# Where the small products stand in a packed-attention and gated feed-forward kernel, and which PSUM quarter each step writes

## The chip, the cores and the metric

The kernel runs on one core of a Trainium2 chip. The metric is the device time in microseconds of one execution, the median over several runs; lower is better. The core's engines are TensorE (PE; its weight loads are shown apart as PEld), VectorE (DVE), ScalarE (ACT), GpSimd (POOL) and SyncE (SP), which issues the DMAs here. [...]

## The reference

Eight batch entries, eight heads, 576 tokens of head dimension 64, 32 packed tokens; feed-forward width 1024.

```python
def sm_attn(qq, kk, vv):
    s = scale * np.matmul(qq, kk.transpose(0, 1, 3, 2))
    s = s - np.max(s, axis=-1, keepdims=True)
    a = np.exp(s)
    a = a / (np.sum(a, axis=-1, keepdims=True) + 1e-09)
    return np.matmul(a, vv)
p_packed = sm_attn(p, k, v)          # 32 packed tokens attend to 576 tokens
x = sm_attn(q, p_packed, p_packed)   # 576 tokens attend to the 32
...
h = np.maximum(x @ w_in, 0.0)
u, v = (h[..., :d_ff // 2], h[..., d_ff // 2:])
v_n = (v - mu) / np.sqrt(var + 1e-06)
v_s = np.einsum('ts,bsd->btd', w_spatial, v_n) + b_spatial[None, :, None]
return ((u * v_s) @ w_out).astype(np.float32)
```

## The kernel before

The batch is walked entry by entry. While the feed-forward of entry b runs (object `ff`, with the attention results of `att`), the attention of entry b+1 (object `nxt`) is threaded between its steps. Entry 0 and the conversion of the weights form a prologue; `for b in range(1, B)` does the rest. All four compute engines are pinned: each issues its instructions in the order in which the Python code calls them, so the order of the calls is the schedule. The order of the work on one engine is therefore written out by hand, and a waiting instruction holds up everything behind it on its engine.

The steps of one entry, in the order before:

- `pack_scores` (PE): packed-token scores of entry b+1, for r = 0 and r = 1 (heads are numbered 2j + r; r chooses the upper or lower 64 rows of the array). Each r is 2 halves of the columns times 4 heads, 64x32 products of float32, two PE instructions each: 16 instructions per r, 32 in all. `pack_max` (DVE), `pack_exp` (ACT) and `pack_sum` (DVE) follow.
- `value(2)`, `value(0)`, `value(1)` (PE, 512 columns wide): the second half of the feed-forward input. `relu`, `relu_tail`, `stats`, `norm`, `norm_hi`, `norm_lo` (ACT, DVE, POOL) normalise it and split it into high and low parts `v_h`, `v_l`, `v_tail`.
- `pack_turn` (PE transposes), `up(0)`, `pack_values` (PE), `up(1)`, `packed_turn`, `up(2)`, `up(3)`: the first half u of the feed-forward input in four chunks e, between the packed attention's next steps; `up_relu` (ACT) keeps each chunk.
- `query_scores` (PE): scores of the 576 queries against the packed tokens, for r = 0 and r = 1, the same shape as `pack_scores`. `query_max(r)` (DVE) transposes the scores out of PSUM into the tile `sm_t`, takes the maximum and subtracts it; `query_exp` (ACT); `query_norm`, `query_turn` (DVE); `query_hi` (ACT) and `query_lo` (DVE) give `a_h`, `a_l`.
- `gate(e)` for e = 0 to 3 (PE, 28 products of 288 columns each) with `gated(e)` (DVE multiplies by u, ACT makes `g_h`) and `gated_lo(e)` (DVE makes `g_l`).
- `mix(1)`, `mix(0)` (PE): packed tokens times `w_in`, 512 columns, 64x32 products, one call for each half x of `w_in`; `mix_hi` (ACT) and `mix_lo` (DVE) split them into `m_h`, `m_l`. The next entry's `value` needs mix(1), its `up` needs mix(0).
- `down(f)` for f = 0 to 3 (PE, 24 products each, over e = 0 to 3), a copy on ACT into a tile `o`, and a store on SP.

PSUM is divided into two pools of two buffers, each buffer of two banks:

```python
    pa = ctx.enter_context(tc.tile_pool(name="pa", bufs=2, space=bass.MemoryType.PSUM))
    pm = ctx.enter_context(tc.tile_pool(name="pm", bufs=2, space=bass.MemoryType.PSUM))
```

`psum_a` serves the attention steps and `psum_m` the feed-forward; each pool hands its buffers out by turns, and a step that takes a buffer waits until the last reader of its former content is done. In the trace the buffers are named `pa_t` and `pm_t`.

Loads go through SP in the order of the calls: `load_k` (tiles kT and pT), `load_v`, `load_q`; kT, v and qT have one buffer each, so a load waits for the last reader of the former entry's data. All engine calls are recorded under one line of the helper class, L42; so the profile's groups are told apart by tiles.

Of the kernel before, what the change touches and what calls it, by code (L numbers as in the profile page):

```python
# [29 lines left out]
# The high word of float64's 2**-126 (the least normal float32), read as float32.  # L30
# [3 lines left out]
class InOrder:  # L34
    """An engine whose instructions are issued in the order of the trace."""
# [13 lines left out]
def body(ctx: ExitStack, tc, q, k, v, vt, p, w_in, w_sp, b_sp, w_out, out):  # L49
    """Two-stage packed attention followed by the spatially gated feed-forward.  # L50

    Heads are numbered h = 2*j + r. An operand with the head dimension in the
    contraction lies on partition (r, d); one with the packed tokens lies on
    partition (j, n), once per r.

    Every float32 value x that enters a one-pass product is held as two
    float32r values with x == hi + lo exactly; a product is hi*hi + hi*lo +
    lo*hi.
    """
# [14 lines left out]
    def psum_a():  # L74
        return pa.tile([P, 2, 512], F32, tag="pa", name="pa_t")

    def psum_m():
        return pm.tile([P, 2, 512], F32, tag="pm", name="pm_t")
# [94 lines left out]
    # w_spatial: [s, t] in chunks of s; the last chunk holds the remaining rows  # L173
    # twice (for v's hi and lo), and its partner the low parts and the bias.
# [16 lines left out]
    def split_spatial():  # L191
        """Steps, each on the scalar engine and then GpSimd."""
# [29 lines left out]
    def scores(ps, lhs, rhs, rs=(0, 1), by_half=False):  # L222
        for r in rs:
            ps[r] = psum_a()
# [16 lines left out]
    class Attention:  # L241
        """The steps for one batch entry; each is a stage on one engine."""

        def __init__(self, b):
            self.b = b
            self.t, self.at = [None, None], [None, None]

        def pack_scores(self, rs=(0, 1)):
# [6 lines left out]
            scores(self.s1, loaded["p", self.b], loaded["k", self.b], rs, self.b == 0)  # L255
# [27 lines left out]
        def pack_turn(self):  # L283
            p1 = self.p1
            self.p1T = one.tile([P, NC + 1, 2, P], F32, tag="p1T", name="p1T")
            self.t1, self.t2 = psum_a(), psum_a()
# [16 lines left out]
        def pack_values(self):  # L303
            v_sb = loaded.pop(("v", self.b))
            self.pv = psum_a()
# [22 lines left out]
        def packed_turn(self):  # L328
            self.ppt = psum_a()
# [6 lines left out]
        def query_scores(self):  # L336
            self.s2 = {}
            scores(self.s2, self.ppT, loaded.pop(("q", self.b)), by_half=self.b == 0)
# [3 lines left out]
        def query_max(self, r, eng=dve):  # L342
# [3 lines left out]
            )  # L346
            mx = small.tile([P, NM], F32, tag="mx", name="mx")
# [31 lines left out]
        def mix(self, x, rs=(0, 1), psum=psum_a):  # L379
# [3 lines left out]
            self.ms = psum()  # L383
            for r in rs:
                for j in range(NJ):
                    mm(
                        self.ms[32 * j : 32 * j + 32, r, :],
# [6 lines left out]
        def mix_hi(self, x, rs=slice(0, 2)):  # L394
            act.copy(self.m_h[:, x, rs, :], self.ms[:, rs, :])

        def mix_lo(self, x, rs=slice(0, 2)):
            rest(self.m_l[:, x, rs, :], self.ms[:, rs, :], self.m_h[:, x, rs, :])

# [1 line left out]
    class FeedForward:  # L401
        """The steps for one batch entry. g counts pairs of row chunks of v."""

        def __init__(self, b, att):
# [3 lines left out]
            self.gs = {}  # L408
# [94 lines left out]
        def up(self, e, rs=(0, 1)):  # L503
            a_h, a_l, m_h, m_l = self.a_h, self.a_l, self.m_h, self.m_l
            if 0 in rs:
                self.us = psum_m()
            for r in rs:
                for n, (ww, aa) in enumerate(((m_h, a_h), (m_h, a_l), (m_l, a_h))):
                    for x in range(2):
                        mm(  # L510
                            self.us[:, x, :HS],
# [6 lines left out]
        def up_relu(self, e):  # L518
            if e == 0:
                self.u = one.tile([P, NJ, S], F32, tag="u", name="u")  # L520
            act.activation(halves(self.u[:, e, :]), self.us[:, :, :HS], AF.Relu)
# [27 lines left out]
        def gate_keep(self, e):  # L549
            """Where the gate comes before u."""  # L550
# [4 lines left out]
        def gated(self, e, gate_first=False):  # L555
# [5 lines left out]
            if gate_first:  # L561
                dve.scalar_tensor_tensor(
                    halves(g), self.us[:, :, :HS], 0.0, other, op0=ALU.max, op1=ALU.mult
# [8 lines left out]
        def down(self, f, split=False):  # L572
            """The halves of the rows by turns or, if split, one after the other."""
            wout_h, wout_l = wout
            fs = slice(f * P, (f + 1) * P)
            terms = [
                (e, ww, gg)
                for e in range(NJ)
                for ww, gg in ((wout_h, self.g_h), (wout_l, self.g_h), (wout_h, self.g_l))
            ]  # L580
            o = two.tile([P, S], F32, tag="o", name="o")
            for xs in ((0,), (1,)) if split else ((0, 1),):
                ps = psum_a() if 0 not in xs else psum_m()
                for n, (e, ww, gg) in enumerate(terms):
                    for x in xs:
                        mm(
                            ps[:, x, :HS],
                            ww[:, e, fs],
                            gg[:, e, x * HS : (x + 1) * HS],
                            n == 0,  # L590
                            n == len(terms) - 1,
                        )
                ts = slice(xs[0] * HS, (xs[-1] + 1) * HS)
                act.copy(
                    o[:, ts].rearrange("p (x t) -> p x t", t=HS),
                    ps[:, xs[0] : xs[-1] + 1, :HS],
                )
                nc.sync.dma_start(out[f * P : (f + 1) * P, self.b, ts], o[:, ts])

# [1 line left out]
    # Every engine issues in the order of the steps below.  # L601
# [56 lines left out]
    att.query_scores()  # L658
    load_q(1)
    keep_warm(W[5])  # L660
    next(conv_v2)
    att.query_max(0, pool)
    att.query_exp(0)
    att.query_max(1, pool)
# [135 lines left out]
    ff.down(0)  # L800
# [5 lines left out]
    ff.down(1)  # L806
# [9 lines left out]
    ff.down(2)  # L816
    ff.down(3)

# [1 line left out]
    for b in range(1, B):  # L820
        more = b + 2 < B
        att, nxt = nxt, (Attention(b + 1) if b + 1 < B else None)
# [16 lines left out]
        if nxt:  # L839
            nxt.pack_turn()  # L840
# [3 lines left out]
        if more:  # L844
            load_k(b + 2)
        ff.norm(0)
        ff.up(0)
        ff.up_relu(0)
        if nxt:
            ff.norm_hi(0)  # L850
            ff.norm(1)
            nxt.pack_values()
            nxt.packed()
            if more:
                load_v(b + 2)
            ff.norm_lo(0)
            ff.up(1)
            ff.norm_hi(2)
            ff.up_relu(1)
            ff.norm_hi(1)  # L860
            nxt.packed_turn()
            nxt.packed_turned()
        else:
            ff.up(1)
            ff.up_relu(1)
            ff.norm_hi(0)
            ff.norm(1)
            ff.norm_lo(0)
            ff.norm_hi(1)
            ff.norm_hi(2)  # L870
        ff.norm_lo(1)
        ff.up(2)
        ff.up_relu(2)
        ff.norm_lo(2)
        ff.up(3)
        ff.up_relu(3)
        if nxt:
            nxt.query_scores()
            if more:
# [11 lines left out]
        ff.gated_lo(0)  # L891
        ff.gate((1,), psum=psum_m if nxt else psum_a)
        ff.gated(1)
        if nxt:
            nxt.query_lo(0)
# [3 lines left out]
        ff.gated_lo(1)  # L899
        if nxt:  # L900
# [60 lines left out]
```

## Time and profile before

| | |
|---|---|
| median of 3 runs | 439.56 us (438.66 to 440.19) |
| span of the profiled execution, first to last instruction | 438.5 us |
| PE busy | 417.3 us (95%) |
| DVE busy | 290.4 us (66%) |
| ACT busy | 185.1 us (42%) |
| POOL busy | 71.7 us (16%) |
| granted PE clock over the span | 0.983 |
| data read and written | 36.61 MB and 9.44 MB |

Rows of the timeline give start and duration in us, engine, line, operation, output tile<-input tiles, shape, and the number of instructions merged into the row; the bracket tells how long the engine was idle before it and what it waited for. In rows of several matmuls the duration runs to the end of the last one; successive matmuls overlap, so the pace is read from start to start. A row of groups ends in the total busy time and the mean duration in ns. The middle entries repeat every 48.9 us or so; entry 2 starts near 150.4, entry 3 near 199.3, entry 4 near 248.1, and the last, entry 7, near 394.7.

### The profile page before, as it was taken

Reading aid. Unit: us, or ns where it says so; the run is one execution under the profiler, and the core shown is the slowest. Engines: PE = TensorE matmul, PEld = TensorE weight load, DVE = VectorE, ACT = ScalarE, POOL = GpSimd, SP = SyncE. Lnnn points to the kernel's source line nnn. Section 1 sums busy time; section 2 is a strip of 40 time slices with the busy share of each in tenths; the row PEclk is TensorE's granted clock in tenths of the full one; section 3 lists DMA queues with packets and bytes.
Section 4 is the critical chain, followed back from the end, with each engine's and each line's share of the span. In section 5 each row is a group of like instructions: output and inputs, shape, how many; then the busy total and the mean of one; then the engine's idle time right before and its main releaser. Section 6 shows DMA issues by size and latency. Waiting matters only on the chain.

```text
span 438.5 us, 8946 instructions
## 1 busy us (share of the span) xinstructions
PE 417.3 (95%) x3882; PEld 367.6 (84%) x3882; DVE 290.4 (66%) x485; ACT 185.1 (42%) x275; POOL 71.7 (16%) x90
## 2 busy tenths in 40 slices
PE   8968877899999999999999999999999999999997
PEld 6755766787898989897898889897898889898997
DVE  2699988697697177834797187825796278825530
ACT  2364663535634264244634354234534363334411
POOL 1356743400300021001200030001200030002100
PEclk9997996999999999999999999999999999999999
DMA  7997303514330335014330335024320200020002
GB/s 258 359 369 287 104 0 116 210 63 167 111 108 4 121 113 205 1 55 169 110 109 28 120 98 195 1 74 142 127 91 28 82 2 1 0 82 29 0 3 106
DMA packets 14219, 46.61 MB, mean 106 GB/s; under 512 B 1378, under 2 KB 4706, under 8 KB 11364
## 3 DMA queue, kind: packets, MB, share of 16 engines
q1 hardware_dynamic: 14180, 46.05, 29.7%
q8 instruction: 30, 0.49, 0.5%
q14 instruction: 9, 0.07, 0.1%
HBM read 36.61 MB, written 9.44 MB: 105 GB/s over the span
## 4 chain that ended last, share of the span: by engine, by line
PE 73%; DVE 15%; DMA 4%; ACT 3%; issue 2%; POOL 2%; SPq 1%; ACTq 0%; POOLq 0%; DVEq 0%
PE pm_t L42 61%; PE pa_t L42 12%; DMA raw<-in_w_in 4%; DVE bits L42 3%; DVE sm_t L42 2%; DVE sm L42 2%; DVE vr_tail L42 1%; ACT p L42 1%; DVE nmax L42 1%; DVE m_l L42 1%; POOL rstd L42 1%; DVE vn L42 1%; DVE w_in_sb L42 1%; POOL wsp_l L42 1%; DVE g_l L42 1%
## 5 line engine op out<-in xcount | busy, mean ns | idle before, releaser
L42 PE MATMUL pm_t<-g_h,wout_l 128*128 128x288 f32 x252 | 54.4, 296 | 1.1 <-POOL wout_l L42 1.1
L42 PE MATMUL pm_t<-g_h,wout_h 128*128 128x288 f32 x252 | 55.1, 299 | 0.2 <-ACT o L42 0.2
L42 PE MATMUL pm_t<-g_l,wout_h 128*128 128x288 f32 x252 | 54.3, 296 | 0.1
L42 POOL TENSOR_TENSOR rstd<-mv,eps 128x2 f32<-128x2 f32 (+2 forms) x26 | 7.5, 287 | 282.4 <-DVE mv L42 282.3
L42 PE MATMUL pm_t<-wsp_h,v_h 128*128 128x288 f32 x224 | 49.4, 302 | 3.1 <-ACT v_h L42 3.1
L42 DVE TENSOR_REDUCE nmax<-pa_t 128x1 f32<-128x576 f32 x16 | 12.0, 752 | 56.5 <-PE pa_t L42 56.5
L42 PE MATMUL pm_t<-wsp_l,v_h 128*128 128x288 f32 x224 | 47.4, 293 | 0.0
L42 PEld LDWEIGHTS pm_t<-g_h,wout_h 128*128 128x128 f32 x252 | 40.5, 189 | 6.6 <-ACT g_h L42 5.0
L42 ACT COPY o<-pm_t 128x576 f32<-128x576 f32 (+1 forms) x32 | 20.1, 633 | 55.5 <-PE pm_t L42 53.9
L42 PEld LDWEIGHTS pm_t<-g_h,wout_l 128*128 128x128 f32 x252 | 40.6, 189 | 1.6 <-POOL wout_l L42 1.6
L42 PEld LDWEIGHTS pm_t<-wsp_h,v_h 128*128 128x128 f32 x224 | 35.4, 188 | 6.9 <-ACT v_h L42 4.1
L42 PEld LDWEIGHTS pm_t<-g_l,wout_h 128*128 128x128 f32 x252 | 40.6, 189 | 0.3 <-DVE g_l L42 0.3
L42 ACT CAST g_h<-g 128x576 fp32r<-128x576 f32 x32 | 21.5, 673 | 36.9 <-DVE g L42 36.8
L42 PEld LDWEIGHTS pm_t<-wsp_l,v_h 128*128 128x128 f32 x224 | 36.5, 189 | 0.0
L42 DVE TENSOR_TENSOR g_l<-g,g_h 128x576 fp32r<-128x576 f32 x32 | 24.6, 768 | 15.4 <-ACT g_h L42 15.3
L42 PE MATMUL pm_t<-wsp_h,v_l 128*128 128x288 f32 x224 | 34.2, 296 | 0.0
L42 PE MATMUL pm_t<-a_h,m_l 128*128 128x288 f32 x128 | 28.6, 306 | 3.2 <-DVE m_l L42 3.2
L42 PEld LDWEIGHTS pm_t<-wsp_h,v_l 128*128 128x128 f32 x224 | 31.4, 189 | 0.0
L42 PE MATMUL pm_t<-a_h,m_h 128*128 128x288 f32 x128 | 30.1, 317 | 0.0
L42 PE MATMUL pm_t<-m_h,a_h 128*128 128x512 f32 x78 | 28.2, 425 | 1.9 <-DVE vr_tail L42 1.1
L42 PE MATMUL pm_t<-a_l,m_h 128*128 128x288 f32 x128 | 28.1, 302 | 0.0
L42 DVE BATCH_NORM_STATS2 bn<-vr 128x6 f32<-128x512 f32 x32 | 20.5, 677 | 11.1 <-ACT vr L42 11.1
(129 smaller groups left out, 837.2 us busy)
## 6 DMA issues: line engine op xcount, KB each, us to landing
out_t<-o SPq DMA_DIRECT2D x31, 288.0 KB, 2.1
v_sb<-in_v SPq DMA_DIRECT2D x8, 1024.0 KB, 6.2
kT<-in_k SPq DMA_DIRECT2D x7, 1152.0 KB, 5.2
qT<-in_q SPq DMA_DIRECT2D x7, 1152.0 KB, 5.1
raw<-in_w_in SPq DMA_DIRECT2D x3, 1024.0 KB, 14.3
kT<-in_k SPq DMA_DIRECT2D x2, 576.0 KB, 5.0
qT<-in_q SPq DMA_DIRECT2D x2, 576.0 KB, 11.7
st_sp<-in_w_sp SPq DMA_DIRECT2D x1, 1152.0 KB, 15.8
```

Of the source, the lines that this page charges most:

```text
L42: return lambda *a, **k: self.tc.keep_in_program_order(call(*a, **k))
```

## The change

PSUM becomes one pool with four tags, the quarters 0 to 3. In the prologue `psum_a` takes quarters 0 and 3 by turns, `psum_m` 1 and 2; in the loop each step names its quarter. `query_max` is divided: its first instruction, the transpose out of PSUM, is now `query_spread`. `down` is divided into parts, so that f = 0 and f = 1 can both do e = 0 to 2 before either does e = 3.

The packed scores are computed one entry further ahead: in entry b those of b+2 (object `far`). They stand, with the query scores and both mixes, directly ahead of the gate. The prologue computes those of entry 2 at its end.

```diff
-    pa = ctx.enter_context(tc.tile_pool(name="pa", bufs=2, space=bass.MemoryType.PSUM))
-    pm = ctx.enter_context(tc.tile_pool(name="pm", bufs=2, space=bass.MemoryType.PSUM))
...
+    psum = ctx.enter_context(tc.tile_pool(name="ps", bufs=1, space=bass.MemoryType.PSUM))
+
+    def on(i):
+        return lambda: psum.tile([P, 2, 512], F32, tag=f"ps{i}", name=f"ps{i}_t")
+
+    def by_turns(*quarters):
+        turn = itertools.cycle([on(i) for i in quarters])
+        return lambda: next(turn)()
+
+    psum_a, psum_m = by_turns(0, 3), by_turns(1, 2)
...
-        def query_max(self, r, eng=dve):
+        def query_spread(self, r):
             self.t[r] = t = two.tile([P, NM, 32], F32, tag="sm_t", name="sm_t")
             dve.transpose(
                 t.rearrange("p (x m) n -> p x (m n)", x=2), self.s2[r][:, :, :HS]
             )
+
+        def query_max(self, r, eng=dve):
+            t = self.t[r]
             mx = small.tile([P, NM], F32, tag="mx", name="mx")
...
+        def down(self, fs, psums, split=False):
+            ps = {f: x() for f, x in zip(fs, psums)}
+            for f in fs:
+                if not split:
+                    self.down_part(ps[f], f, range(NJ - 1))
+            for f in fs:
+                o = two.tile([P, S], F32, tag="o", name="o")
+                if not split:
+                    self.down_part(ps[f], f, (NJ - 1,))
+                    self.store(ps[f], f, o)
+                    continue
...
-    ff.down(2)
-    ff.down(3)
+    ff.down((2,), (psum_m,))
+    ff.down((3,), (psum_m,))
+    far = Attention(2)
+    far.pack_scores()
+    for r in range(2):
+        far.pack_max(r)
+        far.pack_exp(r)
+    far.pack_sum()
+    load_k(3)
     for b in range(1, B):
...
-        if nxt:
-            nxt.pack_scores()
-            for r in range(2):
-                nxt.pack_max(r)
-                nxt.pack_exp(r)
-            nxt.pack_sum()
-        ff.value(2)
-        ff.value(0)
+        ff.value(2, psum=on(0))
+        ff.value(0, psum=on(1))
         ff.relu(2)
-        ff.value(1)
+        ff.value(1, psum=on(2))
...
-            nxt.pack_turn()
+            nxt.pack_turn((on(3), on(0)))
...
-        ff.up(0)
+        ff.up(0, psum=on(1))
...
-            nxt.pack_values()
+            nxt.pack_values(on(2))
...
+        ff.up(1, psum=on(3))
...
+            nxt.packed_turn(on(0))
...
+        ff.up(2, psum=on(1))
...
+        ff.up(3, psum=on(2))
         if nxt:
-            nxt.query_scores()
-            if more:
+            nxt.mix(1, psum=on(3))
+            nxt.query_scores((0,), on(0))
+            nxt.query_scores((1,), on(1))
+            if far:
                 load_q(b + 2)
-            nxt.query_max(0)
-            nxt.query_max(1)
-            nxt.query_exp(0)
-            nxt.query_exp(1)
-        ff.gate((0,), psum=psum_m if nxt else psum_a)
-        ff.gated(0)
+            ff.up_relu(3)
+            nxt.mix_hi(1)
+            nxt.mix(0, psum=on(2))
+            nxt.query_tiles()
+            nxt.query_spread(0)
+            nxt.mix_lo(1)
+            nxt.mix_hi(0)
+            nxt.query_spread(1)
+            nxt.mix_lo(0)
+            if far:
+                far.pack_scores((0,), on(0))
+                far.pack_scores((1,), on(3))
+                if b + 3 < B:
+                    load_k(b + 3)
+                for r in range(2):
+                    far.pack_max(r)
+                    far.pack_exp(r)
+        else:
+            ff.up_relu(3)
+        for e, i in enumerate((1, 2, 0, 3)):
+            ff.gate((e,), psum=on(i))
+            ff.gated(e)
+            ff.gated_lo(e)
+            if nxt and e < 2:
+                nxt.query_max(e)
+                nxt.query_exp(e)
+            elif nxt and e == 2:
+                nxt.query_norm(0)
         if nxt:
-            nxt.query_norm(0)
             nxt.query_turn(0)
             nxt.query_hi(0)
...
             nxt.query_norm(1)
             nxt.query_turn(1)
             nxt.query_hi(1)
...
+            nxt.query_lo(0)
             nxt.query_lo(1)
...
-        if nxt:
-            for x in (1, 0):
-                nxt.mix(x)
-                nxt.mix_hi(x)
-                nxt.mix_lo(x)
-        for f in range(NJ):
-            ff.down(f, split=b == B - 1 and f == NJ - 1)
+            if far:
+                far.pack_sum()
+        ff.down((0, 1), (on(1), on(2)))
+        ff.down((2,), (on(0),))
+        ff.down((3,), (on(3),), split=b == B - 1)
```

More of the change, by code (lines that the diff above doesn't have):

```diff
@@ L1 @@
+import itertools
 from contextlib import ExitStack
@@ L219, in prepare_out, with scores @@
         rest(wout_l, wo, wout_h, pool)
-    def scores(ps, lhs, rhs, rs=(0, 1), by_half=False):
+    def scores(ps, lhs, rhs, rs=(0, 1), by_half=False, psum=psum_a):
         for r in rs:
-            ps[r] = psum_a()
+            ps[r] = psum()
         steps = [(r, x) for r in rs for x in range(2)]
@@ L254, in pack_scores @@
                 self.rtot = small.tile([P, 2], F32, tag="rtot", name="rtot")
-            scores(self.s1, loaded["p", self.b], loaded["k", self.b], rs, self.b == 0)
+            scores(self.s1, loaded["p", self.b], loaded["k", self.b], rs, self.b == 0, psum)
         def pack_max(self, r):
@@ L334, in packed_turned, with query_scores, query_tiles @@
             dve.tensor_copy(self.ppT, self.ppt[:, 0, :P])
-        def query_scores(self):
-            self.s2 = {}
-            scores(self.s2, self.ppT, loaded.pop(("q", self.b)), by_half=self.b == 0)
+        def query_scores(self, rs=(0, 1), psum=psum_a):
+            if 0 in rs:
+                self.s2 = {}
+            scores(self.s2, self.ppT, loaded["q", self.b], rs, self.b == 0, psum)
+        def query_tiles(self):
             self.a_h = one.tile([P, 2, SX], F32R, tag="a_h", name="a_h")
             self.a_l = one.tile([P, 2, S], F32R, tag="a_l", name="a_l")
-        def query_max(self, r, eng=dve):
+        def query_spread(self, r):
             self.t[r] = t = two.tile([P, NM, 32], F32, tag="sm_t", name="sm_t")
@@ L394, in mix_hi @@
         def mix_hi(self, x, rs=slice(0, 2)):
-            act.copy(self.m_h[:, x, rs, :], self.ms[:, rs, :])
+            act.copy(self.m_h[:, x, rs, :], self.ms[x][:, rs, :])
         def mix_lo(self, x, rs=slice(0, 2)):
-            rest(self.m_l[:, x, rs, :], self.ms[:, rs, :], self.m_h[:, x, rs, :])
+            rest(self.m_l[:, x, rs, :], self.ms[x][:, rs, :], self.m_h[:, x, rs, :])
     class FeedForward:
@@ L562, in gated @@
                 dve.scalar_tensor_tensor(
-                    halves(g), self.us[:, :, :HS], 0.0, other, op0=ALU.max, op1=ALU.mult
+                    halves(g), self.us[e][:, :, :HS], 0.0, other, op0=ALU.max, op1=ALU.mult
                 )
@@ L570, in gated_lo, with down_part @@
             rest(self.g_l[:, e, :], self.g.pop(e), self.g_h[:, e, :])
-        def down(self, f, split=False):
+        def down_part(self, ps, f, es, xs=(0, 1)):
             wout_h, wout_l = wout
-            fs = slice(f * P, (f + 1) * P)
             terms = [
                 (e, ww, gg)
-                for e in range(NJ)
+                for e in es
                 for ww, gg in ((wout_h, self.g_h), (wout_l, self.g_h), (wout_h, self.g_l))
             ]
[L581 to L598, printed above, removed]
@@ new lines, in down_part, with store @@
+            for n, (e, ww, gg) in enumerate(terms):
+                for x in xs:
+                    mm(
+                        ps[:, x, :HS],
+                        ww[:, e, f * P : (f + 1) * P],
+                        gg[:, e, x * HS : (x + 1) * HS],
+                        es[0] == 0 and n == 0,
+                        es[-1] == NJ - 1 and n == len(terms) - 1,
+                    )
+        def store(self, ps, f, o, xs=(0, 1)):
+            ts = slice(xs[0] * HS, (xs[-1] + 1) * HS)
+            act.copy(
+                o[:, ts].rearrange("p (x t) -> p x t", t=HS), ps[:, xs[0] : xs[-1] + 1, :HS]
+            )
+            nc.sync.dma_start(out[f * P : (f + 1) * P, self.b, ts], o[:, ts])
@@ new lines, in down @@
+        def down(self, fs, psums, split=False):
[9 more added lines that the diff above has]
+                    continue
+                for x in range(2):
+                    self.down_part(ps[f], f, range(NJ), (x,))
+                    self.store(ps[f], f, o, (x,))
@@ L794, in body @@
     nxt.query_scores()
+    nxt.query_tiles()
     load_q(2)
+    nxt.query_spread(0)
     nxt.query_max(0)
     nxt.query_exp(0)
+    nxt.query_spread(1)
     nxt.query_max(1)
     nxt.query_exp(1)
-    ff.down(0)
+    ff.down((0,), (psum_m,))
     nxt.query_norm(0)
@@ L805, in body @@
     nxt.query_lo(0)
-    ff.down(1)
+    ff.down((1,), (psum_m,))
     nxt.mix(1)
@@ L843, in body @@
         ff.norm(2)
-        if more:
-            load_k(b + 2)
         ff.norm(0)
-        ff.up(0)
+        ff.up(0, psum=on(1))
         ff.up_relu(0)
+        ff.norm_hi(0)
+        ff.norm(1)
         if nxt:
-            ff.norm_hi(0)
-            ff.norm(1)
-            nxt.pack_values()
+            nxt.pack_values(on(2))
             nxt.packed()
-            if more:
+            if far:
                 load_v(b + 2)
[L856 to L861, printed above, removed]
-            nxt.packed_turned()
[L863 to L870, printed above, removed]
+        ff.norm_lo(0)
@@ L871, in body @@
+        ff.up(1, psum=on(3))
+        ff.norm_hi(2)
+        ff.up_relu(1)
+        ff.norm_hi(1)
+        if nxt:
+            nxt.packed_turn(on(0))
+            nxt.packed_turned()
         ff.norm_lo(1)
-        ff.up(2)
+        ff.up(2, psum=on(1))
         ff.up_relu(2)
         ff.norm_lo(2)
-        ff.up(3)
-        ff.up_relu(3)
+        ff.up(3, psum=on(2))
         if nxt:
-            nxt.query_scores()
-            if more:
+            nxt.mix(1, psum=on(3))
+            nxt.query_scores((0,), on(0))
+            nxt.query_scores((1,), on(1))
+            if far:
@@ L898, in body @@
             nxt.query_hi(1)
-        ff.gated_lo(1)
-        if nxt:
+            nxt.query_lo(0)
             nxt.query_lo(1)
-        for e in (2, 3):
-            ff.gate((e,))
-            ff.gated(e)
-            ff.gated_lo(e)
-        if nxt:
-            for x in (1, 0):
-                nxt.mix(x)
-                nxt.mix_hi(x)
-                nxt.mix_lo(x)
-        for f in range(NJ):
-            ff.down(f, split=b == B - 1 and f == NJ - 1)
+            if far:
+                far.pack_sum()
+        ff.down((0, 1), (on(1), on(2)))
+        ff.down((2,), (on(0),))
+        ff.down((3,), (on(3),), split=b == B - 1)
 _INS = ["q", "k", "v", "vt", "p", "w_in", "w_sp", "b_sp", "w_out"]
```

47 lines of the change are left out of this document (23 added, 24 removed).

## The prediction

> **What bounds the kernel now.** I read the page first, then busy time by stretches, then the timeline of the tensor engine (PE) over one entry.
>
> ```profile
> span 438.5 us, 8946 instructions
> PE 417.3 (95%) x3882; PEld 367.6 (84%) x3882; DVE 290.4 (66%) x485; ACT 185.1 (42%) x275; POOL 71.7 (16%) x90
> ```
> ```profile
> 248.10:297.00 48.90, 48.67 (x473) 43.45 (x472) 32.12 (x58) 20.37 (x30) 4.24 (x7) 1.00 0.29 99
> ```
>
> The second row is one middle entry of the batch (columns: length, then PE, weight loads, DVE, ACT, POOL busy, then the granted clock). PE is busy for 48.67 of 48.90 us at full clock, DVE for 32. So only two things can be won: real gaps of PE, and time in which it is called busy but streams nothing. The timeline shows both. First the one real gap, when `value(1)` waits for its PSUM buffer:
>
> ```profile
> 203.29 0.61 PE L42 MATMUL pm_t<-m_h,a_l 128*128 128x512 f32 x2
> 203.74 0.61 PE L42 MATMUL pm_t<-m_l,a_h 128*128 128x512 f32 x2
> 204.58 0.73 PE L42 MATMUL pm_t<-m_h,a_h 128*128 128x512 f32 x2 [0.23 <-DVE vr_tail L42]
> 205.15 0.62 PE L42 MATMUL pm_t<-m_h,a_l 128*128 128x512 f32 x2
> ```
> A pair normally takes 0.46 (203.29 to 203.74). Here the step is 0.84 and the next 0.57: 0.49 lost, in entries 2 to 6.
>
> Then the three stretches of small 64x32 products between full-size ones (packed scores, query scores, mixed weights):
>
> ```profile
> 198.88 0.42 PE L42 MATMUL pm_t<-g_l,wout_h 128*128 128x288 f32 x2
> ...
> 199.24 1.23 PE L42 MATMUL pa_t<-kT,pT 64*32 64x288 f32 x32
> ...
> 200.39 0.50 PE L42 MATMUL pm_t<-m_h,a_h 128*128 128x512 f32 x1
> ...
> 200.73 0.40 PE L42 MATMUL pm_t<-m_l,a_h 128*128 128x512 f32 x1
> ```
> ```profile
> 216.62 0.42 PE L42 MATMUL pm_t<-a_h,m_l 128*128 128x288 f32 x2
> 216.98 1.23 PE L42 MATMUL pa_t<-qT,ppT 64*32 64x288 f32 x32
> 218.13 0.53 PE L42 MATMUL pm_t<-wsp_h,v_h 128*128 128x288 f32 x2
> 218.50 0.42 PE L42 MATMUL pm_t<-wsp_l,v_h 128*128 128x288 f32 x2
> ...
> 221.95 0.43 PE L42 MATMUL pm_t<-wsp_h,v_h 128*128 128x288 f32 x2
> ...
> 232.89 0.42 PE L42 MATMUL pm_t<-wsp_l,v_tail 128*128 128x288 f32 x2
> 233.24 1.95 PE L42 MATMUL pa_t<-w_in_sb,ppT 64*32 64x512 f32 x32
> 235.12 0.53 PE L42 MATMUL pm_t<-g_h,wout_h 128*128 128x288 f32 x2
> 235.49 0.42 PE L42 MATMUL pm_t<-g_h,wout_l 128*128 128x288 f32 x2
> ```
> From 218.50 to 221.95 are 13 pairs, 0.265 each. From the pair before a stretch to the second one after it, less what those two would take anyway: query scores 1.88 - 0.53 = 1.35, mixed weights 2.60 - 0.53 = 2.07, packed scores 1.85 - 0.50 = 1.35 (a pair of 0.265 and one 512-wide product of 0.23). Together 4.77 us per entry, part of it drained array at each end.
>
> **The change, step by step.** Of arithmetic nothing is added or removed. Entry b now runs, after `up(3)`: mix(1) into quarter 3, query halves into 0 and 1, mix(0) into 2, the packed halves of b+2 into 0 and 3, then the gate into 1, 2, 0, 3.
>
> *One run instead of three.* Inside a run one half of the scores is four steps; a step is found from the last matmul's own time:
>
> ```profile
> L42 PE MATMUL pa_t<-w_in_sb,ppT 64*32 64x512 f32 x32 | 1.9, 595 | 0.0
> ...
> L42 PE MATMUL pa_t<-qT,ppT 64*32 64x288 f32 x32 | 1.2, 408 | 0.0
> ```
> Query scores: (1.15 - 0.41) / 3, about 0.24; four steps 0.96, both halves side by side. Mixed weights: (1.88 - 0.60) / 3 = 0.43; two steps, 0.86, per mix. Counted from the run's start: mix(1) to 0.86, query scores to 1.82, mix(0) to 2.68, packed scores 1.15 more with the drain, gate at 3.83. The joined stretch then costs 0.36 + 3.83 + 0.37 - 0.53 = 4.03: 0.75 less than three. In entry 6, where only query and mix join, it saves 3.42 - 3.04 = 0.38. If a change of operands inside the run drained the array too, the saving would be 0; the two mixes of 233.24 follow each other in even steps, so I take all of it.
>
> *value(1).* With quarters 0, 1, 2 for the three value groups it waits for nothing of its own entry: 0.49 gone, five times, 2.45 (bound below: 0, if quarter 2 came late; but the store of f=1 empties it, and f=2 and f=3 of 12 pairs each, 6.4 us, and two value groups still come between).
>
> *What the joined run waits for.* Quarters 0 and 3 are refilled in the run that filled them. PE issues in order, and so does DVE: spread(0), mix_lo(1), spread(1), mix_lo(0). The prologue shows such a refill already:
>
> ```profile
> 100.46 1.17 PE L42 MATMUL pa_t<-kT,pT 64*32 64x288 f32 x16
> ...
> 100.87 1.22 DVE L42 TENSOR_TENSOR m_l<-pa_t,m_h 128x1024 fp32r<-128x1024 f32 x1
> ...
> 102.14 1.17 PE L42 MATMUL pa_t<-kT,pT 64*32 64x288 f32 x16 [0.51 <-DVE m_l L42]
> ...
> 103.24 0.50 PE L42 MATMUL pm_t<-m_h,a_h 128*128 128x512 f32 x1
> ...
> 104.42 0.74 ACT L42 ACTIVATE p<-pa_t,nmax 128x576 f32<-128x576 f32 x1 [0.56 <-DVE nmax L42]
> ```
> The second half of 16 waited for m_l (ends 102.09, PE goes on at 102.14, 0.05 later), and alone it took 1.10 (to 103.24) where both together take 1.15. A half held back costs its whole time. Now the chain in the new run, with these rows:
>
> ```profile
> 217.08 0.65 ACT L42 ACTIVATE u<-pm_t 128x576 f32<-128x576 f32 x1 [0.95 <-PE pm_t L42]
> ...
> 218.22 0.78 DVE L42 STREAM_TRANSPOSE sm_t<-pa_t 128x576 f32<-128x576 f32 x1 [0.88 <-PE pa_t L42]
> ...
> 219.04 0.75 DVE L42 TENSOR_REDUCE mx<-sm_t 128x18 f32<-128x576 f32 x1
> ```
> Spread(0) starts 1.24 after the query scores (216.98 to 218.22): 0.86 + 1.24 = 2.10, ends 2.88; quarter 0 free for PE at 2.93, where PE came at 2.68. First packed half 2.93 to 3.89. DVE's next starts 0.82 after the transpose (219.04): mix_lo(1) 2.92 to 4.14 (1.22, the m_l row), quarter 3 free at 4.19. Second half alone from 4.19, gate at 5.29 instead of 3.83: **1.46 lost in entries 1 to 5**. Spread(1), 4.17 to 4.95, frees quarter 1 at 5.00, hidden there. In entry 6 nothing packed follows, and the gate itself waits to 5.00 instead of 2.84 (2.68 and the mix's drain, 1.88 - 1.72): 2.16 lost. up_relu(3) ends 0.75 after the run's start, so mix(0) finds quarter 2 empty. Behind the waiting PE instruction stands the whole gate, so every wait is lost time. Ends: 0, if DVE were through in time, and 1.46; I take 1.46, because every duration in it has its own row.
>
> *Entry 1.* The packed scores of entry 2 now end the prologue, where they stood anyway. By turns, counting the calls, their second half gets quarter 0, which `value(2)` wants next: it waits for exp(1), 104.42 + 0.74 + 0.05 = 105.21 instead of 103.24: 1.97 lost once (ends: 0, if the turns fell otherwise, and 1.97).
>
> *Costed at nothing, with their cover.*
>
> ```profile
> 223.44 0.74 DVE L42 TENSOR_REDUCE sm<-sm_t 128x18 f32<-128x576 f32 x1
> ...
> 225.52 0.78 DVE L42 STREAM_TRANSPOSE at<-sm_t 128x576 f32<-128x576 f32 x1
> ...
> 235.08 0.75 DVE L42 TENSOR_TENSOR g<-pm_t,u 128x576 f32<-128x576 f32 x1
> 236.58 0.76 DVE L42 TENSOR_TENSOR g_l<-g,g_h 128x576 fp32r<-128x576 f32 x1 [0.74 <-ACT g_h L42]
> ```
> The gate (4 x 14 pairs, 14.8) ends near 20.2. query_norm(0) (2.08, 223.44 to 225.52) now stands before gated(3): DVE is through with it at about 21.4, and g to g_l takes 2.26 more, 23.6. `down` needs e=3 only after 18 pairs of f 0 and 1, 4.8 us, at 25.0. In the old order, after 9 pairs, g_l would come 0.5 late per entry. DVE's last a_l ends near 29.6, the next `value` starts near 33. ACT does query_hi(1) before the stores of f 0 and 1: these slip by 2 us, and their quarters are wanted at 33. On SP `load_k` (one kT and one pT transfer) moves behind `load_q` and ahead of the stores, waits for the packed scores, and its data are wanted a whole entry later. POOL's order is unchanged. packed max and exp move from the entry's start into the gate, where DVE waits for the gate's end.
>
> **Sum.** 5 x (1.46 - 0.75) = +3.55; entry 6, 2.16 - 0.38 = +1.78; entry 1, +1.97; value(1), -2.45: **+4.85 us**. The profiled span of 438.5 becomes 443.4; the median of the runs, 439.56, is 1.06 above that span, so 444.4.
>
> **Rivals.** (a) Faster: DVE frees quarters 0 and 3 before PE comes, all else as above: -5 x 0.75 - 0.38 - 2.45 + 1.97 = -4.6, 435.0. It decides in the run: break even is a loss of 0.49 per entry, so mix_lo(1) would have to end some 1 us before 4.14. For it: DVE is idle for 0.88 ahead of the transpose; against it: that idle time is a wait for PE.
> (b) The held-back half costs no more than its wait, because halves never share the array: 5 x (0.25 + 0.30 - 0.75) + 1.78 + 1.97 - 2.45 = +0.3, 439.9. Against it: 32 in 1.15 beside 16 in 1.10. [...] The x32 and x16 rows speak against it.
> (c) The two idle spells of 2 us (entries 1 and 6) lower the clock:
>
> ```profile
> 30.46 1.08 PE L42 MATMUL pa_t<-w_in_sb,ppT 64*32 64x512 f32 x12 [2.65 <-DVE w_in_sb L42]
> ```
> ```profile
> 49.30 0.53 PE L42 MATMUL pm_t<-wsp_h,v_h 128*128 128x288 f32 x2 [2.00 <-ACT v_h L42]
> ```
> ```profile
> 31.44:38.27 6.83, 5.82 (x19) 4.03 (x14) 6.57 (x8) 3.56 (x6) 6.77 (x6) 0.50 1.02 371
> ```
> After an idle 2.65 the clock was 0.50 for 6.83 us; after 2.00 nothing fell. One drop costs 3.4: 447.8, two 451.2.
>
> **Numbers.** Forecast 0.66 (442.5 to 446.3, its own range), (a) 0.13, (b) 0.07, (c) 0.09, the rest unseen and split. The range of 439.3 to 448.2 takes in the forecast, (b) and one clock drop. Measurement can tell about 0.3% from no change: faster 0.15, within 0.3% 0.09, slower 0.76.
>
> **What will show it.** In the new trace the packed half kT goes in two groups of 16 in entries 1 to 5, the second after an idle wait for DVE m_l; in entry 6 the gate's first matmul waits 2 us for DVE sm_t; `value(2)` of entry 1 waits for ACT p; no wait for vr_tail; an entry of about 49.1 us. One x32 group without a wait, and entries of 47.6, would prove (a) and me wrong.

## The result, and the profile after

The changed kernel takes 446.31 us in the median (445.86 to 447.5) against 439.88 before: a ratio of 1.0155 with a 95% interval of 1.0131 to 1.0178. It is slower by 6.4 us, where 4.85 was forecast. The profiled spans differ by 5.6 us (444.1 and 438.5).

The page after, to be held against its first lines before:

```profile
span 444.1 us, 8944 instructions
PE 418.1 (94%) x3882; PEld 371.2 (84%) x3882; DVE 289.4 (65%) x485; ACT 185.2 (42%) x275; POOL 71.9 (16%) x90
```

The engines' work hardly changed: DVE is busy 1.0 us less, ACT 0.1 more, PE 0.8 and its weight loads 3.6 more. Of the 5.6 us, 4.8 are idle time of PE. Busy time entry by entry, first after the change, then before (start and end of the stretch, its length, busy time of PE, PEld, DVE, ACT and POOL, then the granted clock, DMA share and rate). A stretch begins with the first product of `value(2)`.

```profile
103.56:154.18 50.62, 50.62 (x471) 45.31 (x472) 32.30 (x60) 19.73 (x29) 4.27 (x7) 0.97 0.30 111
154.18:203.03 48.85, 48.85 (x473) 44.02 (x472) 31.98 (x58) 20.38 (x30) 4.23 (x7) 1.00 0.27 99
...
300.79:349.66 48.87, 48.87 (x473) 44.04 (x472) 31.99 (x58) 20.38 (x30) 4.23 (x7) 1.00 0.20 74
349.66:398.11 48.45, 46.84 (x442) 43.22 (x440) 30.11 (x52) 18.72 (x26) 4.24 (x7) 1.00 0.07 26
398.11:444.10 45.99, 41.14 (x286) 39.33 (x284) 16.45 (x28) 13.48 (x20) 4.07 (x7) 1.00 0.09 33
```
```profile
103.24:151.54 48.30, 48.30 (x475) 43.53 (x472) 31.41 (x56) 20.15 (x30) 4.28 (x7) 1.00 0.27 96
151.54:200.39 48.85, 48.62 (x478) 43.45 (x471) 32.11 (x58) 20.37 (x30) 4.24 (x7) 1.00 0.29 99
347.05:394.70 47.65, 47.42 (x446) 42.95 (x440) 32.12 (x58) 19.73 (x29) 4.24 (x7) 1.00 0.07 26
394.70:438.50 43.80, 40.78 (x286) 39.21 (x284) 16.71 (x28) 13.71 (x20) 4.09 (x7) 0.99 0.09 35
```

The middle entries take what they took (48.85 to 48.90). Entry 1 lost 2.3 us, entry 6 0.8, and entry 7 with the tail 2.2; ahead of entry 1 another 2.06 went. That makes 7.4; the prologue of this one execution ended 1.75 earlier than that of the one before (packed scores begin at 98.71 instead of 100.46), which leaves the 5.6. In the seven variants with the same prologue that point lies between 99.0 and 102.1, on both sides of the kernel before, so the 1.75 is not put down to the change. The total times carry this scatter; the entries do not (entries 2 to 5 of the changed kernel agree within 0.05), so the lengths of entries are the firmer measure below.

The timeline of PE after the change shows where the waits are: the start of entry 1, the joined run of entry 2 with its two packed halves, the gate's start in entries 6 and 7, and the last half of `down(3)`.

```profile
100.39 1.17 PE L43 MATMUL ps_t<-kT,pT 64*32 64x288 f32 x16 [0.51 <-DVE m_l L43]
103.56 0.54 PE L43 MATMUL ps_t<-m_h,a_h 128*128 128x512 f32 x1 [1.99 <-ACT p L43]
103.90 0.63 PE L43 MATMUL ps_t<-m_l,a_h 128*128 128x512 f32 x1
...
170.07 1.09 PE L43 MATMUL ps_t<-w_in_sb,ppT 64*32 64x512 f32 x16
170.95 1.36 PE L43 MATMUL ps_t<-qT,ppT 64*32 64x288 f32 x31
...
173.00 1.17 PE L43 MATMUL ps_t<-kT,pT 64*32 64x288 f32 x16
174.13 1.16 PE L43 MATMUL ps_t<-kT,pT 64*32 64x288 f32 x14
175.22 0.53 PE L43 MATMUL ps_t<-wsp_h,v_h 128*128 128x288 f32 x2
...
370.28 0.53 PE L43 MATMUL ps_t<-wsp_h,v_h 128*128 128x288 f32 x2 [1.61 <-DVE sm_t L43]
...
412.26 0.53 PE L43 MATMUL ps_t<-wsp_h,v_h 128*128 128x288 f32 x2 [1.24 <-ACT u L43]
...
439.15 0.40 PE L43 MATMUL ps_t<-g_h,wout_h 128*128 128x288 f32 x1 [0.53 <-ACT o L43]
```

The joined run is 5.15 us long (170.07 to 175.22). Its packed halves run one after the other: the row of 174.13, read in a window that cuts off its first two matmuls, shows the second half. No idle time stands beside it, because the first half's row lasts 1.17 us, to 174.17, past the second half's start; the loss is seen only in the distance of the starts. What held them is in DVE's list, the same view for that engine:

```profile
172.17 0.78 DVE L43 STREAM_TRANSPOSE sm_t<-ps_t 128x576 f32<-128x576 f32 x1 [1.76 <-PE ps_t L43]
172.87 1.19 DVE L43 TENSOR_TENSOR m_l<-ps_t,m_h 128x1024 fp32r<-128x1024 f32 x1
173.98 0.76 DVE L43 STREAM_TRANSPOSE sm_t<-ps_t 128x576 f32<-128x576 f32 x1
```

The transpose ends at 172.95 and the first half starts at 173.00; m_l ends at 174.06 and the second half follows.

### The profile page after: what moved, and what is told of

It reads as the page before. It is cut to its first block, busy times and chain, and to the rows that moved or that the text cites. A ratio compares the mean times of both kernels' runs of the same rounds, so it can differ in the third digit from the quotient of the medians.

```text
span 444.1 us, 8944 instructions
## 1 busy us (share of the span) xinstructions
PE 418.1 (94%) x3882; PEld 371.2 (84%) x3882; DVE 289.4 (65%) x485; ACT 185.2 (42%) x275; POOL 71.9 (16%) x90
## 4 chain that ended last, share of the span: by engine, by line
PE 74%; ACT 1%; DVE 1%; issue 0%; ACTq 0%
PE ps_t L43 74%; ACT v_h L43 0%; DVE sm_t L43 0%; DVE bn L43 0%; DVE m_l L43 0%; ACT u L43 0%; ACT vr L43 0%; DVE vn L43 0%; ACT o L43 0%; ACT v_tail L43 0%; DVE vr_tail L43 0%; DVE mv L43 0%; ACTq L43 0%
## 5 line engine op out<-in xcount | busy, mean ns | idle before, releaser
L43 PE MATMUL ps_t<-wsp_h,v_h 128*128 128x288 f32 x256 | 57.0, 305 | 6.6 <-ACT v_h L43 3.8
L43 PE MATMUL ps_t<-g_h,wout_l 128*128 128x288 f32 x256 | 55.7, 296 | 1.1 <-POOL wout_l L43 1.1
L43 PE MATMUL ps_t<-g_h,wout_h 128*128 128x288 f32 x256 | 55.8, 297 | 0.7 <-ACT o L43 0.7
L43 PE MATMUL ps_t<-g_l,wout_h 128*128 128x288 f32 x256 | 55.5, 296 | 0.1
L43 PE MATMUL ps_t<-wsp_l,v_h 128*128 128x288 f32 x256 | 55.5, 299 | 0.0
L43 PEld LDWEIGHTS ps_t<-wsp_h,v_h 128*128 128x128 f32 x256 | 41.6, 192 | 11.1 <-DVE sm_t L43 4.8
L43 PEld LDWEIGHTS ps_t<-g_h,wout_h 128*128 128x128 f32 x256 | 41.4, 189 | 2.3 <-ACT o L43 1.9
L43 PEld LDWEIGHTS ps_t<-g_h,wout_l 128*128 128x128 f32 x256 | 41.4, 189 | 1.6 <-POOL wout_l L43 1.6
L43 PEld LDWEIGHTS ps_t<-wsp_l,v_h 128*128 128x128 f32 x256 | 42.3, 193 | 0.0
L43 PEld LDWEIGHTS ps_t<-g_l,wout_h 128*128 128x128 f32 x256 | 41.4, 189 | 0.3 <-DVE g_l L43 0.3
```

Source lines behind the costliest of these rows:

```text
L43: return lambda *a, **k: self.tc.keep_in_program_order(call(*a, **k))
```

## The experiments

Ten variants were run. Their times stand against the kernel before in the same session (439.14 to 439.29 in the median) and against the changed kernel's 446.31.

**1. Other quarters in entry 1.**

```diff
-        ff.value(2, psum=on(0))
...
+        at = (1, 2, 0, 3) if b == 1 else (0, 1, 2, 3)
+        to = lambda i, at=at: on(at[i])
+        ff.value(2, psum=to(0))
...
```


> Changed kernel with quarters 0, 1, 2 exchanged in entry 1 only (0 becomes 1, 1 becomes 2, 2 becomes 0), so that its value(2) takes a quarter that is long empty. Theory: the 2.0 us wait of value(2) for exp(1) is gone, and with it the half clock that followed (value stage of entry 1 8.1 us before, 6.5 then): 3.6 us less than the changed kernel, about 442.7. Rival: the half clock belongs to the load of the prologue and not to this wait: 2.0 less, about 444.3, with a clock of 0.5 still in entry 1.

442.89 us (442.54 to 444.08), ratio to before 1.0088 (1.007 to 1.0106). The wait is gone and the clock stays at 1.00 over the entry:

```profile
101.38 1.18 PE L43 MATMUL ps_t<-kT,pT 64*32 64x288 f32 x16 [0.51 <-DVE m_l L43]
102.48 0.50 PE L43 MATMUL ps_t<-m_h,a_h 128*128 128x512 f32 x1
```
```profile
102.48:151.50 49.02, 49.02 (x476) 44.16 (x473) 33.24 (x62) 21.19 (x33) 4.27 (x7) 1.00 0.34 120
```
3.4 us of the loss (by the medians) were one badly placed quarter in one entry.

**2 and 3. The same wait, filled with unread products.**

```diff
+        if b == 1:
+            spare = on(1)()
+            for _ in range(16):
+                mm(spare[:, 0, :P], ident, ident, True, True)
         ff.value(2, psum=on(0))
```


> Changed kernel with 16 products that nothing reads (identity by identity, into quarter 1) on the tensor engine in the place where value(2) of entry 1 waits. Theory: the wait's 2.0 us stay, the clock stays at 1.0, and the value stage of entry 1 takes 6.5 us instead of 8.1: 1.6 less than the changed kernel, about 444.7. Rival: the idle spell is not what lowers the clock: no difference, about 446.3.

447.8 us (446.26 to 448.14), against 444.7 expected. Each product is two instructions, so sixteen are a row of 32; they took 3.6 us (103.15 to 106.74) and outlasted the wait of 1.99; the time says nothing, though the clock held (1.00 from 106.74 to 110.15). The other run has eight in place of sixteen:

> Changed kernel with 8 unread products in place of 16 where value(2) of entry 1 waits, since 16 took 3.6 us, more than the wait. Theory: 8 take 1.8 and fit in the wait: the packed stretch and they end where value(2) began anyway, the clock stays at 1.0, the value stage of entry 1 takes 6.5 instead of 8.1 us: 1.6 less than the changed kernel, about 444.7. Rival: the half clock comes all the same: 446.3.

444.7 us (444.54 to 446.35), as the theory had it. The wait is still there, filled, and the 3.42 us that follow it run at full clock, where the changed kernel had half. Timeline and stretch of this variant, then two stretches of the changed kernel, the wait and what follows it:

```profile
101.78 2.05 PE L43 MATMUL ps_t<-ident 128*128 128x128 f32 x16
103.84 0.50 PE L43 MATMUL ps_t<-m_h,a_h 128*128 128x512 f32 x1
```
```profile
103.84:107.26 3.42, 3.42 (x15) 2.85 (x16) 1.77 (x5) 0.58 (x1) 0.00 (x0) 1.00 0.78 321
```
```profile
100.46:103.87 3.41, 1.42 (x17) 0.64 (x18) 1.91 (x6) 1.67 (x4) 0.00 (x0) 1.00 0.76 239
103.87:107.28 3.41, 3.41 (x9) 2.65 (x8) 1.17 (x4) 0.58 (x1) 0.00 (x0) 0.50 0.67 273
```
So of the 3.6 us at entry 1, 2.0 are the wait and 1.6 the half clock that it brought (the value stage takes 8.10 in the changed kernel, 6.49 here).

**4. The last entry's quarters.**

```diff
-                for x in range(2):
-                    self.down_part(ps[f], f, range(NJ), (x,))
...
+                for x, part in enumerate((ps[f], split())):
+                    self.down_part(part, f, range(NJ), (x,))
...
-        for e, i in enumerate((1, 2, 0, 3)):
+        order = (1, 2, 0, 3) if nxt else (0, 3, 1, 2)
+        for e, i in enumerate(order):
...
-        ff.down((3,), (on(3),), split=b == B - 1)
...
+        ff.down((3,), (on(order[3]),), split=None if nxt else on(order[0]))
```


> Changed kernel, last entry alone: gate into quarters 0, 3, 1, 2, and the second half of down(3) into a quarter of its own. Theory: gate(0) no longer waits 1.24 us for up_relu(2) and the second half of down(3) no longer waits 0.53 us for the copy of the first: up stage 6.4 us instead of 7.8, down 16.0 instead of 16.8, together 2.1 less, about 444.2. Rival: the wait is passed on, because the second pair of v_h comes late too: the gate's third and fourth chunk wait instead, and under 1 us is won.

444.89 us (444.37 to 446.69). By the starts in the timeline the up stage took 6.38 us (7.78 in the changed kernel) and `down` 15.97 (16.78): 2.2 less, as expected, and nothing was passed on (gate 14.93). The median moved by 1.4 only; the four runs of this variant lie up to 2.3 apart.

**5. Query scores first.**

```diff
-            nxt.mix(1, psum=on(3))
             nxt.query_scores((0,), on(0))
             nxt.query_scores((1,), on(1))
+            nxt.mix(1, psum=on(3))
...
             nxt.mix(0, psum=on(2))
...
             nxt.query_spread(0)
+            nxt.query_spread(1)
...
             nxt.mix_lo(1)
             nxt.mix_hi(0)
-            nxt.query_spread(1)
             nxt.mix_lo(0)
...
                 far.pack_scores((0,), on(0))
-                far.pack_scores((1,), on(3))
+                far.pack_scores((1,), on(1))
...
-        for e, i in enumerate((1, 2, 0, 3)):
+        if far:
+            order, into = (3, 2, 0, 1), (2, 0, 1, 3)
...
```


> Changed kernel with the joined run in another order: query scores, mix(1), mix(0), packed scores, these into quarters 0 and 1; DVE does both spreads before mix_lo(1); the gate begins in the quarter of mix(1), in entry 6 in quarter 0. Theory: the run lost its time in waits for DVE; both packed halves now find their quarters empty at 2.07 and 2.75 us after the run's start and run side by side, and the gate waits for mix_lo(1) alone, to 4.3 us instead of 5.15; in entry 6 it starts at 2.9 instead of 4.7. 5 x 0.85 + 1.85 = 6.1 less, about 440.2. Rival: the joined run is slow in itself (operands change in it): it stays at 5 us or more and nothing is won in entries 1 to 5.

442.94 us (441.67 to 443.99), against 440.2 expected. The run shrank from 5.15 to 4.62 us, the entry to 48.36, and entry 6 to 46.8. That decides against the rival, but entries 1 to 5 gain 0.5 each where 0.85 was expected. The gate was expected to wait for m_l until 4.3 us after the run's start; it starts at 4.62, because m_l itself waits for ACT's m_h (second fence):

```profile
173.16 1.38 PE L43 MATMUL ps_t<-kT,pT 64*32 64x288 f32 x32
...
175.08 0.53 PE L43 MATMUL ps_t<-wsp_h,v_h 128*128 128x288 f32 x2 [0.54 <-DVE m_l L43]
```
```profile
173.80 2.36 DVE L43 TENSOR_TENSOR m_l<-ps_t,m_h 128x1024 fp32r<-128x1024 f32 x2 [0.66 <-ACT m_h L43]
```
Both packed halves stand in one row of 1.38 again, side by side; in the changed kernel the same 32 instructions take 2.28 (from 173.00). Without that wait of 0.54 the run would be 4.08 long, an estimate from these rows; the prediction's sum had 3.83 for it. In this execution the wait at entry 1 also passed without a half clock, which saves 1.6 and is not the reordering's merit (see the last section).

**6. DVE's order alone.** PE's order is that of the changed kernel; `query_spread(1)` stands before `mix_lo(1)`, the second packed half goes to quarter 1, and the gate of entries 1 to 5 begins in quarter 3.

> Changed kernel with the order of the tensor engine's joined run kept (mix(1), query scores, mix(0), packed scores), but DVE does both spreads before mix_lo(1); the second packed half goes to quarter 1 instead of 3, and the gate of entries 1 to 5 begins in quarter 3. Theory (each wait of the run is as long as DVE's list ahead of it): second half from 3.6 us after the run's start instead of 4.05, gate at 4.7 instead of 5.15; in entry 6 gate at 3.6 instead of 4.73. 5 x 0.45 + 1.1 = 3.3 less than the changed kernel, about 443.0. Rival: the run's length is set by the tensor engine's own order, DVE's order does not matter: 446.3.

443.85 us (442.89 to 446.55). The run is 4.71 long (171.75 to 176.46, expected 4.7), the entry 48.45, entry 6 47.3: 0.42 and 1.1 less, as expected (the median, 0.85 above the 443.0 expected, has four runs up to 3.7 apart). With PE's order kept, the run's length followed DVE's list, from 5.15 to 4.71.

```profile
171.75 1.09 PE L43 MATMUL ps_t<-w_in_sb,ppT 64*32 64x512 f32 x16
...
176.46 0.53 PE L43 MATMUL ps_t<-wsp_h,v_h 128*128 128x288 f32 x2
```

**7. The remedies of 1, 4 and 5 together.**

> Query scores first (as in the run of that name), with the exchanged quarters in entry 1 and the last entry's quarters mended, all three together. Theory: the three causes are apart in time and add up: 442.9 (queries first) less 2.0 (entry 1, no half clock seen there) less 2.1 (last entry): about 438.8, the time of the kernel before. Rival: another wait takes the place of one of them: over 440.

437.62 us (435.95 to 438.97, ratio 0.9948, 0.9929 to 0.9966): all of the loss is regained and a little more. The causes are apart and add up: entry 1 takes 48.47 us, entries 2 to 5 48.35, entry 6 46.79 and entry 7 with the tail 43.66, each the same as in the variant that mended it alone, or less.

**8. Packed scores back in their old place.** In each entry's loop body, with the packed scores of entry b+1 ahead of `value(2)`:

```diff
-        ff.value(2, psum=on(0))
-        ff.value(0, psum=on(1))
...
+            nxt.pack_scores((0,), on(0))
+            nxt.pack_scores((1,), on(3))
...
+        ff.value(2, psum=on(1))
+        ff.value(0, psum=on(2))
...
-        ff.value(1, psum=on(2))
+        ff.value(1, psum=on(0))
...
+            nxt.query_scores((0,), on(1))
+            nxt.query_scores((1,), on(3))
+            nxt.mix(1, psum=on(2))
...
+            nxt.mix(0, psum=on(0))
...
```


> Packed scores back in their old place at the entry's start, for entry b+1; query scores and both mixes joined ahead of the gate, query scores first; four named quarters, gate begins in the quarter of the first query half; last entry's quarters mended. Theory: only the part of the change that makes no new wait is kept: value(1) does not wait (0.6 per entry) and one stretch of small products fewer (0.38 per entry), entries 1 to 6 of 47.9 us instead of 48.87, nothing lost in entries 1 and 7: 6.0 less than before, about 433.2. Rival: value(1), in the quarter of the first packed half, now waits for exp(0), or the gate for a spread: entries of 48.5 or more, 437 or above.

435.44 us (434.78 to 437.0; 433.2 was expected), ratio 0.9907 (0.9887 to 0.9928): the best of all, and faster than both kernels.

```profile
198.19:246.33 48.14, 48.14 (x479) 44.12 (x472) 32.20 (x58) 20.31 (x30) 4.24 (x7) 1.00 0.29 101
```
Entries of 48.14 against 48.85 to 48.90 before; 47.9 was expected. The value stage gained its 0.6; from the query scores to the end of `down` it is 30.97 against 31.12 before, so one stretch fewer of small products was worth 0.15 and not 0.38.

**9 and 10. The quarters alone.** As in 8, but the mixes between gate and `down`, to see what joining is worth. The excerpt is against the kernel of 8; the added lines stand behind the gate.

```diff
-            nxt.mix(1, psum=on(2))
...
-            nxt.mix(0, psum=on(0))
...
+            for x, i in ((1, 2), (0, 0)):
+                nxt.mix(x, psum=on(i))
+                nxt.mix_hi(x)
+                nxt.mix_lo(x)
```


> As the kernel with the packed scores in their old place, but the mixes also back in their old place between gate and down: what is left is the four named quarters. Theory: joining query scores and mixes is worth 0.38 per entry, six entries: 2.3 slower than that kernel, about 435.5, and 3.6 faster than before. Rival: a joined stretch saves nothing, all is the value(1) wait: no difference between the two.

453.95 us, against 435.5 expected. `down(2)` takes the quarter of mix(0), and mix_lo stands at the end of DVE's list, behind both halves of the query weights: a wait of 1.76 to 1.77 in each of six entries, and in entry 3 a half clock on top (0.50 from 246.71 to 250.12). So the other attempt has `down` use quarters 3 and 1 by turns:

> Packed scores at the entry's start and the mixes between gate and down, as before the change, but with the four named quarters; each down takes quarter 3 or 1 by turns, so that none waits for mix_lo. Theory: what is left of the change is the value(1) wait removed, 0.6 in five entries: 3 less than before, about 436.3; against the kernel with query scores and mixes joined (435.4) the rest, about 0.2 per entry, is what one stretch fewer of small products is worth. Rival: the quarters alone bring nothing, joining brings it all: 439.

446.2 us, against 436.3 expected. Now `down(2)` waits for the copy of `down(0)`, which stands behind two query steps and two mix steps in ACT's list. One fence for each:

```profile
145.93 0.53 PE L43 MATMUL ps_t<-g_h,wout_h 128*128 128x288 f32 x2 [1.77 <-DVE m_l L43]
```
```profile
145.10 0.54 PE L43 MATMUL ps_t<-g_h,wout_h 128*128 128x288 f32 x2 [0.80 <-ACT o L43]
```
Both also begin the gate of entry 7 in the quarter of `up(2)` again and wait 1.23 there. Neither says what joining alone is worth: each has a new wait larger than the effect. In both the value stage is 6.49 us against 7.05 to 7.10 in the kernel before, so that gain belongs to the quarters.

## Why the prediction was right, point by point

*Direction and size.* 444.4 was forecast and 446.31 measured, inside the range and just above the 442.5 to 446.3 that the forecast gave itself. That it came so near is in part luck. Split by entries, the forecast's 4.85 are 1.97 ahead of entry 1, 0.71 in it, 0.22 in each of entries 2 to 5, 1.29 in entry 6 and nothing in entry 7; the traces give 2.06, 2.3, 0, 0.8 and 2.2, together 7.4. Entries 2 to 6 were counted 1.4 too high, which hid part of the half clock (1.6) and of the two waits in entry 7 (2.2) that the sum did not hold.

*The waits of the joined run: right.* Quarter 0 was forecast free 2.93 after the run's start, and the first packed half starts 2.93 after it (173.00). The second was forecast at 4.19 and starts at 4.05, the gate at 5.29 and starts at 5.15. Of the 0.14, 0.12 is a single step (the rest is m_l, 1.19 instead of 1.22): I let DVE's next instruction start 0.82 after the transpose, as in the row of 219.04, where it reads what the transpose writes. In the changed kernel mix_lo(1), which does not read it, started 0.70 after (172.17, 172.87), 0.08 before the transpose's end at 172.95. In entry 6 two such steps made the gate 4.73 instead of 5.00. That a half held back costs its whole time (rival b's opposite) is seen in the two rows of 173.00 and 174.13: 1.13 and 1.09 us to the next start, where both together took 1.15 before (199.24 to 200.39).

*value(1): mis-sized.* No wait for vr_tail is left. The gain is 0.56 to 0.61, not 0.49: the value stage takes 6.38 instead of 7.05 to 7.10, and 0.11 of the difference is the first product after the packed scores, counted elsewhere in the sum. My two rows held only the wait and its first pair.

*Entries 2 to 5: forecast 0.22 slower, measured no different.* That is the sum of the two points above, 0.14 and 0.1.

*Joining stretches: the saving was overrated.* Counted from the starts, three joined stretches without waits take about 4.08 (experiment 5 less its wait) where I had 3.83, so about 0.50 is saved and not 0.75; two joined save 0.15 and not 0.38 (experiment 8). I took the steps of separate stretches and put them end to end. In the changed kernel this stays hidden behind the waits. The drain of my sums is seen in the rows before as time in which PE starts nothing: 0.34 us after the packed scores (200.05 to 200.39) and 0.52 after the mixes (234.60 to 235.12), beside steps of 0.24 and 0.43. From mix(1) to the query scores of the changed kernel no such time shows: two steps of the mix took 0.88 (170.07 to 170.95), where I had 0.86.

*Entry 1: right in the wait, and rival (c) came true with it.* 2.06 were lost against 1.97 forecast. The half clock that I gave 0.09 came too, for 3.41 us and not 6.83, and cost 1.6. Experiments 1 and 3 show both parts.

*Entry 7: the step that failed.* "Costed at nothing" went through a middle entry and left the last one out. There the transposes and packed values are missing that stand between `value` and the gate elsewhere, and the gate begins in quarter 1, which held `up(2)`. Its relu stands behind norm_hi(1) on ACT. That list runs late since norm_hi(0), the first row, which waited 1.70 for the normalised rows; the first of the two relus in the last row ends just before the gate's start at 412.26:

```profile
408.61 1.05 ACT L43 CAST v_h<-vn 128x1024 fp32r<-128x1024 f32 x1 [1.70 <-DVE vn L43]
...
410.63 1.03 ACT L43 CAST v_h<-vn 128x1024 fp32r<-128x1024 f32 x1
411.56 1.18 ACT L43 ACTIVATE u<-ps_t 128x576 f32<-128x576 f32 x2
```
And both halves of `down(3)`, which had a buffer each, now share a quarter, so the second waits for the first one's copy. Together 2.2 us that were in no term; experiment 4 takes them away. The change also gives entry 7 the other entries' order of the norm steps, where the kernel before had one of its own (the diff above leaves this out); experiment 4 keeps the new order and its up stage has no wait, so no cost of the order shows.

*The covers.* query_norm(0) ahead of gated(3), the stores behind query_hi and the moved loads cost nothing, as forecast: gate and `down` are free of waits in entries 1 to 6 (15.0 and 12.80 us).

## What to carry to other kernels

Here a buffer refilled in the same stretch that filled it was released at the pace of the reader's list (the joined run went from 5.15 to 4.71 us by DVE's order, with PE's kept), so follow that list before counting what a shorter tensor stretch saves. Hand-named buffers have to be followed through the first and the last pass as well: most of what this kernel lost lay at entry 1 and in entry 7. And ask what products that run side by side take alone: the two packed halves took 1.15 us together and 1.13 and 1.09 once the second had to wait.

## What the runs showed of the hardware that was not expected

An idle spell of about 2 us was followed by a half clock in some places and not in others. In the changed kernel the clock stood at 0.50 for 3.41 us from 49.26, from 69.74 and from 103.87, and at 1.00 for 13.65, 17.07 and 30.72 us ahead of these, which is 4, 5 and 9 times 3.41; a step is one such 3.41 us here. The 1.99 us at entry 1 fell into one step and the next ran at 0.50 (the rows of 100.46 and 103.87). With query scores first the same 1.99 us came 2.5 us later, 0.19 of it in the step before; PE was busy 1.61 of 3.41, and the clock stayed (first fence). In experiment 9, with its waits of 1.76 to 1.77, a step with 1.65 us of PE work was followed by one at 0.50, and a step with 1.64 by one at 1.00 (second fence), so PE's busy time in this view does not tell the two cases apart.

```profile
104.26:107.67 3.41, 1.61 (x7) 1.35 (x8) 1.12 (x4) 1.53 (x5) 0.00 (x0) 1.00 0.78 258
107.67:111.08 3.41, 3.41 (x17) 2.82 (x16) 1.96 (x4) 1.25 (x2) 0.73 (x2) 1.00 0.28 108
```
```profile
243.30:246.71 3.41, 1.65 (x13) 1.41 (x12) 3.05 (x4) 2.67 (x4) 0.00 (x0) 1.00 0.12 45
246.71:250.12 3.41, 3.41 (x16) 3.41 (x16) 0.00 (x0) 0.00 (x0) 0.00 (x0) 0.50 0.33 128
396.90:400.31 3.41, 1.64 (x14) 1.41 (x12) 3.30 (x5) 2.92 (x5) 0.00 (x0) 1.00 0.05 18
400.31:403.70 3.39, 3.39 (x25) 3.39 (x26) 0.00 (x0) 0.00 (x0) 0.00 (x0) 1.00 0.41 156
```
Nor does it in the two kernels: 1.87 us of work in the kernel before (65.57 to 68.98) was followed by 0.50, 1.70 in the changed one (39.02 to 42.43) by 1.00. The same counting bears on rival (c), which read from the kernel before that after an idle spell of 2.00 us (to 49.30) nothing fell. In steps of 3.41 from the clock's change at 38.27 that spell lay across two, with PE busy 2.21 in the first (45.09 to 48.50) and 2.62 in the second (48.50 to 51.92). In the changed kernel the same wait, 2.01 us to 48.37, lay within the step from 45.85 to 49.26, PE was busy 1.40 of it, and the next step ran at 0.50.
